# Block-sparse attention and an MLP mixer in one kernel: the gates of two batches computed transposed, in groups

## The chip, the cores and the metric

One core of a Trainium2 chip. A core has five engines that run side by side, each with its own queue: TensorE (PE: matmuls; its weight loads are listed as PEld), VectorE (DVE), ScalarE (ACT), GpSimd (POOL) and SyncE (SP), which here only issues transfers. 16 DMA engines move data between HBM (the main memory) and SBUF (the working memory, 128 partitions); TensorE writes to a third memory, PSUM. The metric is the device time of one execution in microseconds (us); the table below gives the median of four runs.

## The reference

Four batches, 8 heads, 768 positions, 64 values per head. Each query may see three of the 12 key blocks of 64 positions, chosen by a gate, and its own block, all of it causal. The result goes through a mixer of two MLPs: one across the 768 positions, one across the 512 channels.

```python
k_rep = k.reshape(B, H, 12, 64, D).mean(axis=3)
gate_scores = np.einsum('bhsd,bhnd->bhsn', q, k_rep)        # causal blocks only
top_idx = np.argsort(gate_scores, axis=-1)[..., -3:]
mask = chosen blocks | own block, and pos_q >= pos_k
attn = softmax(where(mask, scale * q @ k.T, -1e9))
x = (attn @ v), heads side by side                          # (4, 768, 512)
h = np.maximum(x.transpose(0, 2, 1) @ w_tok1, 0) @ w_tok2
u = x + h.transpose(0, 2, 1)
out = u + np.maximum(u @ w_ch1, 0) @ w_ch2
```

## The kernel before

**Pairs.** Two heads of a batch make a pair; there are 16 pairs, four to a batch. For pair i the kernel does the following.

- SP loads k, q and v (`load_qk` L265, two transfers each for k and q; `load_v` L274, one). The load buffers are rings: three for k, three for q (`kl`, `ql`), two for v.
- TensorE transposes k and q with six f32 transposes each (L353) into a PSUM tile `big`, ACT copies them to SBUF as `kt` and `qt` (L362), and GpSimd casts the halves to f16 into `KA` and `Q` (L368) and v into `V16` (L280). `KA` and `Q` have R = 4 slots, used in turn. Below or above the 64 head rows, each slot of `KA` holds 12 indicator rows (1 where a key lies in block n), and the matching 12 rows of `Q` get the mask's bias. So one matmul of 128 rows gives scores and mask together.
- DVE sums k over each block (`ksum` L376) and puts the sums of the two heads side by side into `ks2` (`kcopy` L384).
- The gate (L394): five f32 matmuls, each with 128 columns of `qt` as weights and the 24 columns of `ks2` streamed. DVE adds the causal bias (L402), takes the eight largest of each row of 12 with ten MAX8 (L411), compares with the third largest (L418), and makes the bias in f16, with the query's own block let through by `own` (L426, into `bn16`). TensorE transposes this bias, five f16 transposes (`mask` L437), and DVE copies the 12 rows of each head into `Q` (`put_mask` L445).
- Per head: scores in three tiles (L459), `exp` on ACT (L472), the diagonal blocks masked on DVE (L479; for pair 0 a triangle is added on TensorE, L463), the product with v (`av`, L490) and the normalisation on DVE (L498, L509) into `x16`.

**The MLP** of a batch follows when its four pairs are done: `tok1` (L521, L552 for batch 0), `umix` (L533, L566), the transpose of u (on TensorE for batch 0, by a DMA that SP issues for the others, L344), `ch1` (L602) with ReLU on ACT and DVE (L612, L614), `ch2` (L623), the last add (L631), the store (L635).

**The order.** Every step is an `Op` with an engine, a cost, dependencies, buffers and a priority. `plan()` makes the order of all engines from these before the program is emitted: each engine takes the ready step of the best priority. A pair's preparation has priority `pre = 10 (i - LATER)` (`AHEAD` for the first four), its attention 10 i, the MLP of batch b 1000 (b + 1), so MLP work is taken where attention has nothing ready. SP takes loads strictly by priority. Each engine's queue then runs in that fixed order. Ahead of it `manual_schedule` emits the set-up: constants over ACT's queue (`id32`, `gbias`, `own`, `id16`, `tri`), memsets on DVE and GpSimd, the indicator rows by GpSimd's queue (L875). The MLP weights are loaded by GpSimd's queue too, each behind the cast that `WAIT` names; `w_tok1` and `w_tok2` are the first. `dummy` matmuls (`warm`, L642) fill TensorE before 17 us. The path with `VIA` (k transposed by DMA) is in the code but off: `VIA = 16` is past the last pair.

Of the kernel before, what the change touches and what calls it, by code (L numbers as in the profile page):

```python
# [28 lines left out]
R = 4  # L29
# [3 lines left out]
VIA = 16  # L33
# [3 lines left out]
IDLE = 1e9  # L37
WAIT = [("kt", 3, 1), ("kt", 3, 1), ("qt", 3, 1), ("qt", 3, 1), ("qt", 4, 1), ("qt", 4, 1),
# [29 lines left out]
def plan(ops, rings, near=60.0):  # L68


    free = dict(PE=900.0, ACT=4800.0, DVE=4500.0, POOL=7500.0, SP=750.0, SPO=750.0)
# [106 lines left out]
def kernel(  # L178
# [26 lines left out]
    dram = ctx.enter_context(tc.tile_pool(name="dr", bufs=1, space=bass.MemoryType.DRAM))  # L205
# [3 lines left out]
    RINGS = dict(big=2, bank=3, av=1, ql=3, kl=3, v32=2, qt=2, kt=2, gs=2, e0=3, e1=3, e2=3, rc=2,  # L209
                 x16=3, h1=2, u=2, uT=2, h2=1, ob=3)  # L210
# [19 lines left out]
    K16 = [sp.tile([96, 8, 256], F16, tag=f"K16{y}", name=f"K16{y}") for y in range(2)]  # L230
    ks2 = [sp.tile([128, 2 * NB], FP, tag=f"ks{r}", name=f"ks{r}") for r in range(R)]
    bn16 = [sp.tile([128, NJ, 2, 64], F16, tag=f"bn{r}", name=f"bn{r}") for r in range(R)]
# [3 lines left out]
    wc2_16 = sp.tile([128, NFC, DM], F16, tag="wc2", name="wc2")  # L236
    warm = sp.tile([128, 256], F16, tag="warm", name="warm")
# [46 lines left out]
    def load_k8(i):  # L284
        b, h = pairs[i]

        def f():
            t = sb("kt", [128, 2, 8, D], FP, f"k8_{i}")[0:96]
            T["k8", i] = t
            nc.sync.dma_start(out=t.rearrange("p g t d -> p g (t d)"),  # L290
                              in_=k[b, h:h + 2].rearrange("g (p t) d -> p g (t d)", t=8))
        return f

    def ksum8(i):
        def f():
            t = sp.tile([96, 2, D], FP, tag="kp", bufs=2, name=f"kp_{i}")
            T["kp", i] = t
            nc.vector.tensor_reduce(out=t, in_=T["k8", i].rearrange("p g t d -> p g d t"), axis=AX.X, op=ALU.add)
        return f

    def ksum_pe(i):
        def f():
            p = ps("bank", [128, NB], "kps")
            T["kst", i] = p
            nc.tensor.matmul(out=p, lhsT=T["kp", i].rearrange("p g d -> p (g d)"), rhs=blk, start=True, stop=True)
        return f

    def cast_k8(i):
        def f():
            y = i % 2  # L310
            nc.gpsimd.tensor_copy(out=K16[y].rearrange("p t (g c) -> p g t c", g=4)[:, 0:4:3, :, :], in_=T["k8", i])
        return f

    def store_k(i):
        def f():
            t = dram.tile([S, 256], F16, tag=f"ks{i % 2}", name=f"kscr_{i}")
            T["kscr", i] = t
            nc.sync.dma_start(out=t.rearrange("(p t) c -> p (t c)", t=8), in_=K16[i % 2].rearrange("p t c -> p (t c)"))
        return f

    def turn_k(i):
        return lambda: nc.sync.dma_start_transpose(out=KAX[:, i % R, :, :], in_=T["kscr", i])

    def k16_zero(y):
        return lambda: nc.gpsimd.memset(K16[y].bitcast(FP), 0.0)

    def k16_ind(y):
        def f():
            for c in (64, 128):
                nc.gpsimd.tensor_copy(out=K16[y][:, :, c:c + NB],  # L330
                                      in_=blk.rearrange("p (o n) -> p o n", o=1).broadcast_to([96, 8, NB]))
        return f

    def zero_q(r):
        def f():
            nc.gpsimd.memset(QA[r][0][64:128, :].bitcast(FP), 0.0)
            nc.gpsimd.memset(QA[r][1][0:64, :].bitcast(FP), 0.0)
        return f

# [574 lines left out]
```

## Time and profile before

| what | value |
|---|---|
| median of 4 runs | 273.85 us (273.04 to 274.81) |
| the profiled execution's own time | 274.21 us |
| its span, first to last instruction | 272.4 us, granted clock 1.0 |
| busy PE / DVE / ACT / POOL | 261.6 / 162.1 / 142.3 / 81.3 us |
| gate matmuls L394 (80, recorded as 160) | 19.9 us busy |
| mask transposes L437 (80) | 7.1 us busy |
| HBM read | 27.21 MB |

Busy times of TensorE count each record from its start to its end, and records overlap, so what a matmul costs on the path is the distance between starts and is read from the chain of waits or from a timeline. "Idle before" in a group is the time in which its engine did nothing before an instruction of the group, with what ended it. The profiled execution is one run; it took 0.36 us more than the median.

### The profile page before, as it was taken

How to read it: one execution, taken by the hardware profiler on the slowest of the kernel's cores; microseconds unless marked ns; L12 is line 12 of the kernel's file. 1: busy time of each engine (PE TensorE's matmuls, PEld its weight loads, DVE VectorE, ACT ScalarE, POOL GpSimd, SP SyncE). 2: the span in 40 equal slices, each digit the busy share in tenths (PEclk: the TensorE clock that was granted, in tenths of full speed). 3: DMA queues.
4: the chain of work that ended last, by engine and by line, in shares of the span. 5: the costliest groups of instructions: out<-in, count | busy, mean ns of one | idle time of the engine just before them, and what ended most of it. 6: DMA issues, size and time to landing. Idle time of an engine off the chain costs nothing.

```text
span 272.4 us, 5924 instructions
## 1 busy us (share of the span) xinstructions
PE 261.6 (96%) x2309; PEld 173.9 (64%) x2309; DVE 162.1 (59%) x561; ACT 142.3 (52%) x188; POOL 81.3 (30%) x112
## 2 busy tenths in 40 slices
PE   7799879999999999999999999999999999999994
PEld 5687668886778777676877655644456544466443
DVE  5468947998889788889897633334233262433222
ACT  2366968877888888888477713430014400044000
POOL 8687807555445465337342000000000000000000
PEclk9999999999999999999999999999999999999999
DMA  8999999999999994581611111005420007210032
GB/s 174 199 215 218 150 210 215 199 185 198 222 213 226 204 213 97 110 182 25 117 41 41 38 43 75 0 2 103 145 99 2 0 16 177 84 73 0 2 143 88
DMA packets 92059, 32.31 MB, mean 119 GB/s; under 512 B 85568, under 2 KB 88536, under 8 KB 92032
## 3 DMA queue, kind: packets, MB, share of 16 engines
q1 hardware_dynamic: 87920, 27.53, 46.8%
q0 software_dynamic: 3392, 4.15, 9.2%
q8 instruction: 18, 0.29, 0.5%
q10 hardware_dynamic: 720, 0.25, 0.4%
q14 instruction: 9, 0.07, 0.1%
HBM read 27.21 MB, written 6.29 MB: 123 GB/s over the span
## 4 chain that ended last, share of the span: by engine, by line
PE 81%; DMA 8%; DVE 4%; SPq 2%; ACT 1%; issue 1%; POOL 1%; DVEq 0%; ACTq 0%; POOLq 0%
PE c L623 23%; PE c L602 22%; PE sps L459 10%; PE aps L490 6%; PE gps L394 5%; DMA ql<-in_q_dram 4%; PE ups L533 3%; PE tok L521 3%; PE tql L353 3%; DMA w<-in_moe_w_tok_dram 3%; PE tkl L353 3%; SPq L265 2%; DMA v<-in_v_dram 2%; PE bps L437 1%; ACT e L472 1%
## 5 line engine op out<-in xcount | busy, mean ns | idle before, releaser
L472 ACT ACTIVATE e<-sps 128x1024 f16<-128x1024 f32 (+1 forms) x96 | 84.3, 918 | 17.3 <-PE sps L459 11.9
L602 PE MATMUL c<-uT,wc 128*128 128x256 f16 (+1 forms) x384 | 68.1, 326 | 0.2 <-ACT h L612 0.2
L623 PE MATMUL c<-wc,h 128*128 128x512 f16 (+2 forms) x300 | 65.0, 371 | 0.0
L612 ACT ACTIVATE h<-c 128x512 f16<-128x512 f32 x48 | 28.7, 598 | 68.9 <-PE c L602 61.5
L602 PEld LDWEIGHTS <-wc 128*128 128x128 f16 x384 | 37.0, 98 | 24.6 <-issue 0.4
L459 PE MATMUL sps<-Q,KA 128*128 128x512 f16 (+3 forms) x256 | 50.0, 306 | 1.1 <-ACT e L472 1.0
L623 PEld LDWEIGHTS <-h 128*128 128x128 f16 x300 | 28.7, 98 | 31.4 <-issue 0.6
L614 DVE TENSOR_SCALAR h<-c 128x256 f16<-128x256 f32 x48 | 20.2, 421 | 33.8 <-PE c L602 33.8
L479 DVE TENSOR_TENSOR e<-e,m 128x256 f16<-128x256 f16 x90 | 31.8, 361 | 14.2 <-ACT e L472 13.7
L631 DVE TENSOR_TENSOR ob<-u,c 128x512 f32<-128x512 f16 (+2 forms) x25 | 16.6, 666 | 38.4 <-PE c L623 38.4
L368 POOL CAST KA<-kt 64x768 f16<-64x768 f32 x32 | 27.1, 848 | 28.3 <-ACT kt L362 24.9
L459 PEld LDWEIGHTS <-KA 128*128 128x128 f16 x256 | 22.5, 100 | 15.2 <-issue 1.1
L368 POOL CAST Q<-qt 64x768 f16<-64x768 f32 x32 | 26.7, 833 | 10.9 <-ACT qt L362 9.5
L490 PE MATMUL aps<-V,e 128*128 128x65 f16 x672 | 26.9, 194 | 0.3
L490 PEld LDWEIGHTS <-e 128*128 128x128 f16 x672 | 25.6, 98 | 2.2 <-issue 0.4
L394 PEld LDWEIGHTS gps<-ks,qt 128*128 128x128 f32 x160 | 19.2, 192 | 2.5 <-DVE ks L384 1.3
L280 POOL CAST V<-v 128x768 f16<-128x768 f32 x16 | 13.2, 827 | 25.1 <-DMA v<-in_v_dram 21.0
L394 PE MATMUL gps<-ks,qt 128*128 128x24 f32 x160 | 19.9, 267 | 0.3 <-DVE ks L384 0.2
L362 ACT COPY kt<-tkl 128x768 f32<-128x768 f32 x16 | 12.8, 798 | 11.1 <-PE tkl L353 5.7
L509 DVE TENSOR_TENSOR x<-aps,rc 128x384 f16<-128x384 f32 x32 | 17.6, 550 | 0.5
L445 DVE COPY Q<-bps 12x640 f16<-12x640 f16 x32 | 15.5, 484 | 1.9 <-PE bps L437 0.7
L362 ACT COPY qt<-tql 128x768 f32<-128x768 f32 x16 | 12.8, 798 | 7.0 <-PE tql L353 6.3
(55 smaller groups left out, 217.0 us busy)
## 6 DMA issues: line engine op xcount, KB each, us to landing
kl<-in_k_dram SPq DMA_DIRECT2D x32, 192.0 KB, 5.0
ql<-in_q_dram SPq DMA_DIRECT2D x32, 192.0 KB, 4.6
v<-in_v_dram SPq DMA_DIRECT2D x16, 384.0 KB, 5.4
out_dram<-ob SPq DMA_DIRECT2D x23, 256.0 KB, 2.0
wc<-in_moe_w_ch_dram POOLq DMA_DIRECT2D x8, 384.0 KB, 7.8
w<-in_moe_w_tok_dram POOLq DMA_DIRECT2D x2, 384.0 KB, 8.3
out_dram<-ob SPq DMA_DIRECT2D x1, 160.0 KB, 1.8
KA<-indc POOLq DMA_DIRECT2D x2, 72.0 KB, 4.4
```

The costliest lines, as they stand in the source:

```text
L362: nc.scalar.copy(out=t, in_=p[:, 0:S])
L368: nc.gpsimd.tensor_copy(out=dst[i % R][x][lo:lo + 64, :], in_=T[name, i][lo:lo + 64, :])
L394: nc.tensor.matmul(out=g[:, j, :], lhsT=T["qt", i][:, 128 * j + 128:128 * j + 256], rhs=ks2[i % R], start=True, stop=True)
L459: nc.tensor.matmul(out=p[:, off + a:off + a + n], lhsT=KA[i % R][x][:, 128 * kk:128 * kk + 128], rhs=QA[i % R][x][:, q0 + a:q0 + a + n], s ...
L472: nc.scalar.activation(out=e[:, 0:width], in_=T["sps", i, x, g][:, 0:width], func=AF.Exp, scale=scale)
L479: nc.vector.tensor_tensor(out=d, in0=d, in1=m0, op=ALU.mult)
L490: nc.tensor.matmul(out=p[:, jq, :], lhsT=T["e", i, x, g][:, o:o + 128], rhs=V16[i % (R + 1)][:, x, kk, :], start=(kk == 0), stop=(kk == jq))
L509: nc.vector.tensor_tensor(out=T["x16", b][:, :, 64 * hh:64 * hh + 64], in0=T["aps", i, x][:, :, 0:64], in1=T["rc", i, x].broadcast_to([128 ...
L602: nc.tensor.matmul(out=p, lhsT=wc1_16[:, cc, 128 * fc:128 * fc + 128], rhs=T["uT", b][:, cc, a // 128:e // 128, :], start=(cc == 0), stop= ...
L612: nc.scalar.activation(out=T["h2", b][:, fc, a:e], in_=T["c1", b, fc, n], func=AF.Relu)
L614: nc.vector.tensor_scalar(out=T["h2", b][:, fc, a:e], in0=T["c1", b, fc, n], scalar1=0.0, scalar2=None, op0=ALU.max)
L623: nc.tensor.matmul(out=T["c2", b, j, lo], lhsT=T["h2", b][:, fc, 128 * j:128 * j + 128], rhs=wc2_16[:, fc, lo:hi], start=(fc == 0), stop=( ...
```

## The change

Pairs 0 to 5 keep their gates one by one. Pairs 6 and 7 make a group, 8 to 11 another, 12 to 15 a third (`GROUPED`). For a group the gate is turned round: `ks2` of a pair (24 columns, padded to 32) is the weight and 640 columns of `qt` are streamed, in two matmuls (512 and 128 columns). Pair s of the group uses columns 32 s to 32 s + 31 of the array (`tile_position`) and so writes partitions 32 s and up. ACT copies the result to SBUF (`gate_e`), five f32 transposes turn it back (`gate_b`), and one add, one comparison and one bias serve the group; MAX8 stays at ten per pair. The biases lie packed, 32 columns a pair, in `bn16`, so five f16 transposes give the masks of the whole group. `put_mask` now copies 24 rows (both heads), and the indicator rows of head 1 lie 12 rows further, so that each head picks its own.

With it: R becomes 5, `qt` has four buffers, `x16` two in place of three, `bn16` four in a ring of its own; the bias works on `own4`, in which `own` stands four times; preparation of a group has one priority base (2.5 apart for its pairs, `EXTRA` 5 earlier), v keeps its old one; the code of the `VIA` path goes, with its constant `blk`. In the set-up only slot 0 of `KA` is cleared and gets the indicators from DMA; slots 1 to 4 are copied from it on GpSimd in `zero_q`, which also fills `own4`, except for its first part, which DVE copies behind its memsets of `ks2`.

```diff
-R = 4
+R = 5
+NBN = 4
+EXTRA = 5.0
+GATE = {2: 1150, 3: 1400, 4: 1700}
+GROUPED = [[0], [1], [2], [3], [4], [5], [6, 7], [8, 9, 10, 11], [12, 13, 14, 15]]
...
     RINGS: qt=2 -> 4, gs=2 -> 1, x16=3 -> 2, new: gt=1, gm=1, m8=1, bn=NBN
...
     def zero_q(r):
         def f():
+            for x in range(2):
+                lo = 64 * (1 - x)
+                nc.gpsimd.tensor_copy(out=KAX[lo:lo + 64, r, x, :].bitcast(FP), in_=KAX[lo:lo + 64, 0, x, :].bitcast(FP))
             nc.gpsimd.memset(QA[r][0][64:128, :].bitcast(FP), 0.0)
             nc.gpsimd.memset(QA[r][1][0:64, :].bitcast(FP), 0.0)
+            if r < 4:
+                nc.gpsimd.tensor_copy(out=own4[:, r:4 * GJ:4, :], in_=own)
...
+    def gate_t(gi):
+        def f():
+            p = ps("big", None, "gtp")
+            T["gtp", gi] = p
+            for a, e in ((0, 512), (512, S - 128)):
+                for s, i in enumerate(GROUPED[gi]):
+                    nc.tensor.matmul(out=p[32 * s:32 * s + 32, a:e], lhsT=ks2[i % R],
+                                     rhs=T["qt", i][:, 128 + a:128 + e], start=True, stop=True,
+                                     tile_position=(0, 32 * s))
+    def gate_e(gi):
+            nc.scalar.copy(out=t[0:n, :], in_=T["gtp", gi][0:n, 0:S - 128])
+    def gate_b(gi):
+            for j in range(GJ):
+                nc.tensor.transpose(out=p[:, 128 * j:128 * j + n], in_=T["gt", gi][0:n, 128 * j:128 * j + 128],
+                                    identity=ident32[0:n, 0:n])
...
+    def mask(gi):
+            for j in range(GJ):
+                nc.tensor.transpose(out=p[0:n, 128 * j:128 * j + 128], in_=bn16[gi % NBN][:, j, 0:n], identity=ident16)
-            nc.vector.tensor_copy(out=QA[i % R][x][lo:lo + NB, 128:S], in_=T["bps", i][lo:lo + NB, :])
+            nc.vector.tensor_copy(out=QA[i % R][x][lo:lo + 2 * NB, 128:S], in_=T["bps", gi][32 * s:32 * s + 2 * NB, :])
...
-        pre = 10.0 * (i - (AHEAD if i < FIRST else LATER))
+        pre = 10.0 * (i0 - (AHEAD if i < FIRST else LATER)) + 2.5 * (i - i0) - (0 if len(GROUPED[gi]) == 1 else EXTRA)
+        vpre = 10.0 * (i - (AHEAD if i < FIRST else LATER))
...
         for r in range(R):
             nc.vector.memset(ks2[r], 0.0)
+        nc.vector.tensor_copy(out=own4[:, 0:4 * GJ:4, :], in_=own)
         for x in range(2):
             lo = 64 * (1 - x)
-            for r in range(R):
-                nc.gpsimd.memset(KAX[lo:lo + 64, r, x, :].bitcast(FP), 0.0)
+            nc.gpsimd.memset(KAX[lo:lo + 64, 0, x, :].bitcast(FP), 0.0)
...
-        blk = const("blk", (np.arange(96)[:, None] // 8 == nidx[None, :]).astype(np.float32), FP, nc.gpsimd)
```

The new order keeps TensorE's queue as it was up to the gate of pair 5, apart from the size of the masks. From there on the transposes of pairs 7 and 9 to 15 come earlier; on SP, k and q of pair 7 stand ahead of v of pair 5, k and q of pairs 9 to 11 ahead of v of pairs 7 to 10, and k and q of 12 to 15 ahead of v of 11.

## The prediction

> **What bounds the kernel now.** I read the page's slices first, then the table of stages, then the chain of waits, then the groups of the gate. The slices (TensorE, its granted clock, DMA):
>
> ```profile
> PE   7799879999999999999999999999999999999994
> PEclk9999999999999999999999999999999999999999
> DMA  8999999999999994581611111005420007210032
> ```
>
> TensorE is full from the sixth slice (34 us) to the last one, at full clock; DMA is full for the first 14 slices (95 us). The stage table (stretch, length, busy us of PE, PEld, DVE, ACT, POOL, clock, DMA share, GB/s) says the same with numbers:
>
> ```profile
> 30.00:40.00 10.00, 7.79 (x122) 5.88 (x121) 6.15 (x21) 7.80 (x11) 3.30 (x5) 1.00 1.16 191
> 60.00:70.00 10.00, 9.72 (x125) 7.25 (x123) 8.30 (x33) 7.88 (x11) 5.63 (x7) 1.00 1.13 199
> 90.00:100.00 10.00, 9.95 (x112) 7.79 (x110) 7.57 (x31) 8.97 (x13) 4.24 (x6) 1.00 1.02 205
> 120.00:130.00 10.00, 10.00 (x105) 7.03 (x103) 9.89 (x37) 8.71 (x10) 5.38 (x6) 1.00 0.40 79
> 260.00:272.40 12.40, 8.74 (x53) 4.74 (x51) 2.81 (x5) 0.00 (x0) 0.00 (x0) 1.00 0.29 105
> ```
>
> From 40 us on TensorE idles some 0.5 us up to its last matmul at 268.5 us, because MLP matmuls of finished batches fill what attention leaves. So after 40 us a microsecond of TensorE work saved is a microsecond off the end, whatever ACT or DVE do, as long as no wait takes its place. Before 40 us there is nothing to fill with, and the chain of waits (start, length, what) runs through loads and GpSimd:
>
> ```profile
> 20.91 5.16 DMA v<-in_v_dram
> 26.19 0.84 POOL V L280
> 27.08 0.74 POOL KA L368
> 27.96 0.77 POOL Q L368
> 28.74 7.47 DMA w<-in_moe_w_tok_dram
> 36.25 0.84 PE tok L552 x12
> ...
> 81.21 1.08 PE gps L394 x10
> ```
>
> **The gate, per pair.** The groups by form (busy, mean ns of one, idle before):
>
> ```profile
> L394 PE MATMUL gps<-ks,qt 128*128 128x24 f32 x160 | 19.9, 267 | 0.3 <-DVE ks L384 0.2
> L353 PE MATMUL tkl<-id,kl 128*128 128x128 f32 x96 | 13.3, 275 | 0.7 <-issue 0.7
> L437 PE MATMUL bps<-id,bn 128*128 128x128 f16 x80 | 7.1, 220 | 0.1
> ```
>
> 160 records for 80 gate matmuls: an f32 matmul that is no transpose goes through as two. On the path a gate is 1.08 us (chain above; 1.03 to 1.30 over the pairs) and the five mask transposes 0.28 us. For pairs 6 to 15 that is 10 x 1.08 + 10 x 0.28 = 13.6 us of TensorE, all removed.
>
> **What replaces it on TensorE.** Three groups: a pair and two fours. No row shows column tiles, nor a long f32 stream, so I bound both. Stream: six f32 transposes take 0.66 us, 110 ns for 128 columns or 0.86 ns a column; two records per matmul make 1.72 ns, so 640 columns are 1.10 us (the old gate passed the same 640 columns as weights in 1.08 us). Lowest end: the f16 row, 512 columns each 216 ns, which gives 0.27 us. Overlap of the tiles: from full (one stream) to none (n streams). Each tile's loads I put at 0.1 us (an f32 load of 128 columns is 192 ns, and 32 columns take less; two records). I take full overlap, 1.10 + 0.1 n plus 0.1: 1.3 us for the pair, 1.6 us for a four, since the tiles share neither weights nor output partitions; the other end, no overlap, is 2.4 and 4.8 us. Turning back is five f32 transposes, 0.55 us a group, and a mask 0.28 us a group. Sum: 1.3 + 1.6 + 1.6 + 3 x 0.55 + 3 x 0.28 = 7.0 us. **Saved on TensorE: 6.6 us**; without overlap 0.9 us is lost (2.4 + 4.8 + 4.8 + 2.5 = 14.5 us); at the f16 rate 9.1 us are saved.
>
> A record of a 128x512 f16 matmul lasts 379 ns while the next starts 216 ns later, so 0.16 us of each is tail that the next one covers. The Trainium skill (TensorEngine Tiling (Array Packing), Key Properties) says that a change of tiling mode drains TensorE. By that rule each group would pay the tail on entering and on leaving, 6 x 0.16 = 1.0 us, and the forecast below would be 270.7 instead of 269.7; no row here shows such a switch.
>
> **ACT and DVE.** Three evacuations of 640 columns come to ACT: by the 768-column copy (798 ns) about 0.7 us each. DVE's gate chain shrinks: add, compare and bias of four pairs cost 4 x 0.86 us (277, 305, 278 ns), and at 480 elements about 0.65 us each by the 512-element add of 688 ns. Both are covered by TensorE's fill. But the chain of a four is now one long latency ahead of four pairs: add 0.65, forty MAX8 3.3, compare 0.67, bias 0.65, with some 2 us of other DVE work queued between (reciprocal, output add, two ReLUs, a diagonal), 7.2 to 7.6 us in all. In the new order TensorE has 8.7 us of work between turning back and mask for pairs 8 to 11, and 7.15 us for 12 to 15. I charge **0.5 us** of wait for the second (0 to 1.5).
>
> **Loads, moved on SP's queue.** k and q of pair 7 now go ahead of v of pair 5, those of 9 to 11 ahead of v of 7 to 10. In that stage DMA is the limit (199 GB/s), so a load moves by what it overtakes: v is 0.39 MB, 1.9 us. q of pair 7 was issued at 55.25 and landed 9.9 us later, 65.1; it will land at 63.2. TensorE's new order wants it 6.8 us after the gate of pair 5 (54.5 us), at 61.3, or 62.7 with the late start below: **0.5 us** of wait (0 to 2.5). k of pair 8 overtakes nothing (71.8 us) and is wanted at 72.1; q of pair 8 about 74.5, wanted at 75.0. TensorE took these three about 5 us after they landed (69.97, 76.8 and 78.98 us); now it is under one. k of 11 gains 5.7 us and is early. v of 9 and 10 wait for the two v buffers, with k and q of 12 queued behind them on SP; by bytes k of 12 stays where it was (landed near 95), wanted at 95.6.
>
> **The start.** Timeline of the first microseconds (start, length, engine, what):
>
> ```profile
> 0.75 3.00 POOL L865 MEMSET KA<- 64x384 f32 x8 [0.29 <-POOLq L898]
> 1.91 0.49 ACTq L214 DMA_DIRECT2D own<-ownc  x1
> 6.05 0.96 DVE L376 TENSOR_REDUCE kst<-tkl 128x12 f32<-128x768 f32 x1 [2.02 <-PE tkl L353]
> 7.05 0.80 ACT L362 COPY kt<-tkl 128x768 f32<-128x768 f32 x1 [4.80 <-DMA tri<-tric]
> ```
>
> DVE now copies `own` before most of its memsets, and `own` lands at 6.1 us (4.2 after issue). Behind that wait stand two Q memsets, four bn16 memsets and six V16 memsets, 2.5 us, then the block sums of pair 0: 6.05 becomes about 8.9, ACT's copies wait for that, and the first scores move from 15.0 to about 16.0. GpSimd loses six KA memsets (2.2 us) and gains, per further ring slot, two KA copies (0.41 each, by the memset of the same shape at 1.07 ns an element, as the 768-element cast; 0.82 at most) and an `own` copy (0.2, three times), and a whole fifth slot. Its queue: the indicator DMA lands near 6.6, slots 1 and 2 until 10.6, pair 0's casts until 14.1, then with slots 3 and 4 in between without a gap to the issue of `w_tok1` at 30.1 in place of 28.74. The kernel before left GpSimd 3.5 us of idle between 11 and 27 us (1.10, 1.00, 0.42, 0.59 and 0.43 ahead of its casts), so only 1.4 us of its added work shows. TensorE already waits for this load, so `tok` starts near 37.6 instead of 36.25: **1.4 us lost**, which contains the 1.0 us of the first scores. With copies at 0.82 it is 4.6 us; if DMA, not the issue, times that load, 0.5 us. The dropped `blk` load (0.5 us of GpSimd) is in this.
>
> **Sum.** -6.6 + 0.5 + 0.5 + 1.4 = -4.2 us. The profiled execution took 274.21 us (span 272.4 and 1.8 around it), 0.36 above the median 273.85 and inside the runs' spread (273.04 to 274.81). 274.2 - 4.2 = 270.0; on the median **269.7 us**.
>
> **Rivals.** (a) *The tiles run one after the other.* Then the three gates cost 12.0 instead of 4.5 us, 7.5 us more: 277.2 us, slower. For it: no row here shows two matmuls side by side. Against it: distinct weights, outputs and streams. It decides from the point where the three gates together exceed 8.7 us, about 3.2 us for a four. (b) *They overlap in twos*: 2.6 us a four, 271.7 us. (c) *A wait takes the place*: GpSimd's copies at 0.82 (3.2 us more: 272.9), or the k and q of pairs 7 and 8 late by 2 us and more and the mask chain late in both fours (also about 3 us). For it: margins under 1 us and a full DMA; against it: every one of these is met by the counts above. (d) *Nothing of the start shows and the tiles cost just one stream*: 7.7 saved, 0.5 to 1 lost: 267.0 us. (e) That the gates were hidden anyway and nothing changes I exclude: TensorE is full where they stand.
>
> **How the numbers follow.** Forecast 0.50 (its own range 268.3 to 271.3), (d) 0.10, (b) 0.10, (c) 0.15 (272 to 274.5), (a) 0.15 (274.5 to 278). Range 267.0 to 275.0: below it half of (d), above it most of (a). Measurement tells 0.5%, 1.4 us: faster is below 272.5, slower above 275.2. Faster: 0.50 + 0.10 + 0.08 + 0.06 = 0.74; slower 0.12, from (a) and a little of (c) with it; within 0.14.
>
> **What would show it.** Right: one tiled gate of four spanning 1.2 to 1.9 us, its matmul records overlapping; 0.55 us for turning back; `tok` of batch 0 near 37.6; TensorE full from 40 us; waits on q of pair 7 under 1 us. Wrong: a tiled gate over 3 us, TensorE idle in 57 to 76 us on k or q loads, idle ahead of the masks near 105 or 145 us, or the first `tok` past 39 us.

## The result, and the profile after

The changed kernel takes 273.57 us (median of 54 runs, 270.47 to 278.83), the kernel before 273.47 us (78 runs beside them, 272.51 to 278.37). Over all runs the medians are the same within 0.1 us, where a gain of 4.2 us was forecast. The ratio is 0.997, with an interval of 0.9956 to 0.9984; like all ratios below it is formed only from runs within 1.5% of the fastest of their kernel, which here leaves out 16 of the 54 and 2 of the 78. The profiled execution took 271.72 us (span 270.0, full clock) against 274.21 (span 272.4) before: between these two it is 2.5 us. So there are two gaps to explain: 4.2 against 2.5 us in the profile, and 2.5 us against nothing between the profile and the median of the runs.

The slices of the page (TensorE, its granted clock, DMA) have dips that the kernel before did not have, in slices 13 and 14 of DMA (6 and 4) and in 15 and 18 of TensorE (7 and 6):

```profile
PE   6798999999999979969999999999999999999994
PEclk9999999999999999999999999999999999999999
DMA  8999999999996499967412000006320026310032
```

In the table of stages (columns as in the prediction) they have their sizes. TensorE's busy time from 90 to 120 us was 29.9 of 30 us before (the row of 90 to 100 us stands in the prediction; before, then after):

```profile
100.00:110.00 10.00, 10.00 (x110) 7.68 (x110) 8.45 (x35) 8.51 (x12) 5.95 (x8) 1.00 0.64 137
110.00:120.00 10.00, 9.95 (x105) 7.14 (x103) 7.76 (x28) 8.15 (x11) 4.12 (x5) 1.00 0.51 112
```

```profile
90.00:100.00 10.00, 8.49 (x87) 5.70 (x86) 6.34 (x24) 6.65 (x10) 7.14 (x9) 1.00 0.64 136
100.00:110.00 10.00, 9.80 (x83) 6.83 (x82) 7.68 (x43) 5.11 (x7) 3.63 (x4) 1.00 1.21 223
110.00:120.00 10.00, 7.58 (x59) 4.17 (x58) 9.89 (x19) 6.05 (x8) 5.76 (x7) 1.00 0.91 183
```

After the change that is 4.1 us of idle time. The whole account, from the same table summed over the span:

| us | before | after | difference |
|---|---|---|---|
| TensorE busy | 261.6 | 256.3 | -5.3 |
| TensorE idle up to 40 us | 6.4 | 5.6 | -0.8 |
| TensorE idle from 40 us to its last matmul, and the end | 4.4 | 8.1 | +3.7 |
| span | 272.4 | 270.0 | -2.4 |

What the change was meant to do, it does. TensorE's timeline around the gate of pairs 8 to 11 (start, length, what; in brackets the idle time before it and its releaser):

```profile
94.86 1.28 PE L361 MATMUL gtp<-qt,ks 128*32 128x512 f32 x16
96.08 0.45 PE L455 MATMUL sps<-Q,KA 128*128 128x512 f16 x2
96.36 0.60 PE L598 MATMUL c<-uT,wc 128*128 128x256 f16 x4
96.96 0.77 PE L381 MATMUL gbp<-id,gt 128*128 128x128 f32 x5
99.24 0.85 PE L310 MATMUL tkl<-id,kl 128*128 128x128 f32 x6 [1.51 <-DMA kl<-in_k_dram]
```

Sixteen matmul records in four column tiles take 1.22 us until the next work starts. The pair takes 1.20 (from 65.42 to 66.62), the second four 1.22 (140.67 to 141.89). Twice the tiles add 0.02 us: they overlap fully. But the last line is the first new wait: TensorE waits for k of pair 12. It comes from SP's queue (its timeline; the length is from the first to the last issue of the group):

```profile
78.80 13.83 SPq L276 DMA_DIRECT2D v<-in_v_dram  x4
92.72 1.79 SPq L267 DMA_DIRECT2D kl<-in_k_dram  x2
94.61 2.81 SPq L267 DMA_DIRECT2D ql<-in_q_dram  x2
```

SP stands for 13.8 us at four loads of v, because v of pairs 9 and 10 needs the two v buffers, and GpSimd's casts of v of 7 and 8 free them late (the casts start at 86.1 and 91.4 us). Meanwhile DMA has less to do: slices 13 and 14 of its row fall to 6 and 4. The second new wait is near 118 us, first in TensorE's timeline, then in that of VectorE:

```profile
116.18 0.23 PE L486 MATMUL aps<-V,e 128*128 128x65 f16 x2
116.70 0.27 PE L486 MATMUL aps<-V,e 128*128 128x65 f16 x3 [0.30 <-DVE e L475]
118.95 0.68 PE L486 MATMUL aps<-V,e 128*128 128x65 f16 x16 [1.99 <-DVE e L475]
```

```profile
109.26 4.00 DVE L441 COPY Q<-bps 24x640 f16<-24x640 f16 x8
113.29 0.69 DVE L537 TENSOR_TENSOR u<-x,ups 128x512 f16<-128x512 f16 x1
113.90 2.75 DVE L475 TENSOR_TENSOR e<-e,m 128x256 f16<-128x256 f16 x2
116.57 0.94 DVE L333 TENSOR_REDUCE kst<-kt 128x12 f32<-128x768 f32 x1
117.43 1.27 DVE L537 TENSOR_TENSOR u<-x,ups 128x512 f16<-128x512 f16 x2
118.62 0.48 DVE L475 TENSOR_TENSOR e<-e,m 128x256 f16<-128x256 f16 x2
```

The packed mask of four pairs is ready all at once, so its eight copies into Q stand in one row, 4.00 us, where before two at a time were spread over four pairs. Behind them come two diagonals (L475) of 1.15 and 1.68 us, against a median of 0.29 us for the 90 in this profile, and the third diagonal of pair 8, for which TensorE waits, has a block sum and two u adds ahead of it. The two slow diagonals are 2.2 us longer than usual together, as much as the wait itself. They lie beside six GpSimd casts without a pause (113.3 to 118.2 us). The Trainium skill (GPSIMD Engine Reference, Specifications) says that GpSimd shares its memory interface with VectorE, and that VectorE instructions with two inputs in SBUF contend for it; the trace agrees with that: the 62 of the 90 diagonals with no GpSimd work beside them took 0.294 us at most, and every longer one overlapped some (though not every one that did was longer).

At the start, `own` holds up VectorE as forecast (the chain has 4.59 us of `own` from 1.90 us on; the sum of block 0 begins at 9.2 us, forecast 8.9), and the first gate waits:

```profile
11.71 1.29 PE L351 MATMUL gps<-ks,qt 128*128 128x24 f32 x10 [1.85 <-ACT qt L319]
36.51 0.83 PE L548 MATMUL tok<-x,w 128*128 128x128 f16 x12
```

But the first token matmul starts at 36.51, 0.26 us later than before, not 1.35: `w_tok1` was issued at 30.5, 1.8 us later, and landed 5.7 us after its issue instead of 7.5 (at 36.26 us, before at 36.20).

**Between the profile and the runs.** Each of the 54 runs carries its mean granted clock:

```
mean clock of the run     runs   median us
0.998 to 1.000              11      271.64
0.994 to 0.996              12      272.86
0.988 to 0.992              13      273.73
0.984 to 0.987               6      274.48
0.972 to 0.981              12      276.40
```

A straight line through them gives 271.45 us at full clock and 2.4 us more for each per cent of clock (correlation 0.92). The profiled execution is one of the fastest fifth, with full clock. The kernel before varies less: the middle 80% of its runs lie within 272.7 to 274.8, those of the changed kernel within 271.5 to 276.4. And its clock hardly varies: of 68 runs of it that were taken beside the experiments with their clocks, 66 have 0.997 or more and none less than 0.994. At 0.998 and more the medians are 271.64 us for the changed kernel (11 runs) and 273.56 for the one before (60 runs). So the change gives 1.9 us at full clock, and the clock takes as much from the changed kernel's median; the other 0.7 us of the profile's 2.5 is that the profiled execution before lay 0.7 us above its median.

### The profile page after: what moved, and what is told of

Same layout as the page of the kernel before. It is cut to its first block, busy times and chain, and to the rows that moved or that the text cites. A ratio compares the mean times of both kernels' runs of the same rounds, so it can differ in the third digit from the quotient of the medians.

```text
span 270.0 us, 5718 instructions
## 1 busy us (share of the span) xinstructions
PE 256.3 (95%) x2229; PEld 164.0 (61%) x2229; DVE 161.0 (60%) x544; ACT 141.5 (52%) x191; POOL 83.9 (31%) x118
## 4 chain that ended last, share of the span: by engine, by line
PE 85%; DVE 7%; DMA 3%; ACT 2%; issue 1%; ACTq 0%; SPq 0%
PE c L598 23%; PE c L619 22%; PE sps L455 13%; PE aps L486 8%; PE tql L310 3%; PE tkl L310 3%; PE ups L529 3%; PE tok L517 2%; PE gps L351 2%; DMA own<-ownc 2%; DMA ql<-in_q_dram 2%; DVE Q L441 1%; ACT e L468 1%; PE gtp L361 1%; PE bps L434 1%; DVE e L475 1%
## 5 line engine op out<-in xcount | busy, mean ns | idle before, releaser
L455 PE MATMUL sps<-Q,KA 128*128 128x512 f16 (+3 forms) x256 | 49.0, 306 | 1.0 <-ACT e L468 1.0
L619 PEld LDWEIGHTS <-h 128*128 128x128 f16 x300 | 28.8, 98 | 30.5 <-issue 0.6
L325 POOL CAST KA<-kt 64x768 f16<-64x768 f32 x32 | 26.3, 823 | 47.9 <-ACT kt L319 34.8
L475 DVE TENSOR_TENSOR e<-e,m 128x256 f16<-128x256 f16 x90 | 30.9, 352 | 14.9 <-ACT e L468 14.2
L325 POOL CAST Q<-qt 64x768 f16<-64x768 f32 x32 | 27.4, 856 | 4.2 <-ACT qt L319 2.8
L505 DVE TENSOR_TENSOR x<-aps,rc 128x384 f16<-128x384 f32 x32 | 17.7, 553 | 0.7
L333 DVE TENSOR_REDUCE kst<-kt 128x12 f32<-128x768 f32 x15 | 14.2, 945 | 4.0 <-ACT kt L319 3.7
L441 DVE COPY Q<-bps 24x640 f16<-24x640 f16 x32 | 15.4, 483 | 1.3 <-PE bps L434 0.7
L310 PE MATMUL tkl<-id,kl 128*128 128x128 f32 x96 | 13.3, 275 | 2.6 <-DMA kl<-in_k_dram 1.5
```

Source lines behind the costliest of these rows:

```text
L310: nc.tensor.transpose(out=p[:, 128 * j:128 * j + 128], in_=t[:, j, :], identity=ident32)
L325: nc.gpsimd.tensor_copy(out=dst[i % R][x][lo:lo + 64, :], in_=T[name, i][lo:lo + 64, :])
L441: nc.vector.tensor_copy(out=QA[i % R][x][lo:lo + 2 * NB, 128:S], in_=T["bps", gi][32 * s:32 * s + 2 * NB, :])
L455: nc.tensor.matmul(out=p[:, off + a:off + a + n], lhsT=KA[i % R][x][:, 128 * kk:128 * kk + 128], rhs=QA[i % R][x][:, q0 + a:q0 + a + n], s ...
L475: nc.vector.tensor_tensor(out=d, in0=d, in1=m0, op=ALU.mult)
L619: nc.tensor.matmul(out=T["c2", b, j, lo], lhsT=T["h2", b][:, fc, 128 * j:128 * j + 128], rhs=wc2_16[:, fc, lo:hi], start=(fc == 0), stop=( ...
```

## The experiments

**Theory.** Most of the missing gain is two waits from the new order: (1) k and q of pair 12 behind v on SP; (2) VectorE's eight copies and what stands behind them. Rivals: the waits only pass the time on to each other; the rest of the change (masks, start) costs more than the forecast has; and it is the clock (TensorE's granted clock falls in some runs behind an idle time).

**k and q of pair 12 ahead of v of 9 and 10** (inserted in the planned order):

```diff
+    hold = next(o for o in order if o.prio == 82.0 and o.eng == "SP")
+    for key in (("kl", 12), ("ql", 12)):
+        order.remove(O[key])
+        order.insert(order.index(hold), O[key])
```

> The changed kernel; only on SP's queue k and q of pair 12 stand ahead of v of pairs 9 and 10. Theory A (the gain went into two waits of TensorE: 1.5 and 0.2 us for k and q of pair 12, held on SP behind v of 9 and 10, which wait for their buffers until GpSimd has cast v of 7 and 8; and 2.3 us for the diagonals of pair 8 on DVE): the first wait goes, k of pair 12 lands before 95 us, the span is 1.5 to 2 us shorter (268.0 to 268.5 at full clock). Rival B (the second wait grows by what the first one gives, since the mask chain of pairs 8 to 11 sets both): span within 0.5 us of 270.0. Theory C (the granted clock falls in some runs after an idle stretch of TensorE of 1.5 us or more): runs below clock 0.99 become fewer, the mean clock of the runs rises; if the clock falls for another reason, it stays at about 0.99.

Measured: 273.87 us (5 runs, 270.03 to 277.66), ratio 0.9943 (0.9879 to 1.0008). The wait for k of pair 12 is gone from the table of waits, the wait for the diagonal stays at 2.4 us (the profiled run had a clock of 0.944, so only its waits are read). The time decides nothing by itself. The clocks of the five runs (0.944 to 0.994) did not rise, as the theory of the clock expected.

**The third diagonal of pair 8 ahead of the block sum and the u adds:**

```diff
+    order.remove(O["dg", 8, 0, 2])
+    order.insert(order.index(O["dg", 8, 0, 1]) + 1, O["dg", 8, 0, 2])
```

> The changed kernel; only on DVE's queue the third diagonal of pair 8 stands ahead of the block sums of pair 14 and two adds of u. Theory A: the wait of 2.0 us of the first product with v of pair 8 shrinks to 0.3 to 0.6 us (two diagonals of 1.1 and 1.7 us still stand before it), span 268.3 to 268.8 at full clock. Rival B (another instruction of DVE's queue takes over, such as the adds of u that hold MLP tiles): span within 0.5 us of 270.0. Theory C: one idle stretch fewer, so the mean clock of the runs rises.

Measured: 273.4 us (10 runs), ratio 0.9994 (0.9956 to 1.0031). The table of waits (us in total, times, longest):

```profile
PE aps L486 <- DVE x L505: 1.8, 1, 1.8
PE tkl L310 <- DMA kl<-in_k_dram: 1.6, 1, 1.6
```

The wait for the diagonal is gone, and a wait of 1.8 us for the normalisation of pair 8 (L505) stands in its place: one edit in VectorE's order passes the time on to the next thing in that queue.

**Both together:**

> Both edits of the two runs before. Theory A: their gains add up, span 266.3 to 267.0 at full clock, which is 5.5 us under the kernel before and about what was forecast for TensorE's work plus the start. Theory C: no idle stretch of TensorE over 0.7 us is left past 40 us, so the clock is 1.0 in nearly all runs and the median is within 1 us of the fastest run, 268 to 269 us. If C is wrong, half the runs stay 2 us and more above the fastest.

Measured: 271.32 us (5 runs, 271.06 to 271.76), ratio 0.9932 (0.9912 to 0.9953). Wait (1) is gone, and the normalisation takes 2.3 us. Both theories missed here: the span is 269.7 us and not 266.3 to 267.0, and all five runs have a clock of 0.992 to 0.994 where 1.0 was expected. The profile has one stretch of 3.4 us at half clock, from 13.1 us on, behind the wait of 1.6 us for the first gate: the waits of the middle are not the only ones that matter for the clock.

**The copies of nine to eleven and thirteen to fifteen left out**, on top of both edits (12 of 32 copies; the masks of six pairs are then not applied):

```diff
+            if len(GROUPED[gi]) == 4 and s > 0:
+                return
```

> The run with both edits, and in the two groups of four only the first pair's mask rows are copied: twelve of the 32 copies of mask rows (24 rows x 640, 0.48 us each on DVE) are left out, so the output is not the reference's. Theory A2 (what is left of TensorE's wait in 115 to 123 us, 2.3 us ahead of a product with v, is DVE's backlog behind eight copies in a row, 4.0 us): the wait falls under 0.5 us and the span by 1.5 to 2.5 us against the run with both edits. Rival (the backlog is the six adds of u and GpSimd's casts at the same time, the copies only stand near it): the wait stays above 1.5 us.

Measured: 267.78 us (4 runs, 267.61 to 268.81), ratio 0.9786 (0.9739 to 0.9833), span 265.5 against 269.7 us. TensorE from 105 to 125 us is busy 18.97 us instead of 17.25, so 1.7 of the 4.2 us come from here. The rest lies at the start, where the profiled run with the copies waits 1.6 us for the first gate and has its stretch at half clock, which this run has not. The wait fell to 1.0 us, between the theory (under 0.5) and the rival (over 1.5). So wait (2) comes mostly with the row of copies. Part of that may be the slow diagonals: with the copies the first three of pair 8 stand beside the casts and take 2.95 us, without them they come ahead of most of the casts and take 0.28, 0.29 and 0.43 us. What the copies cost of themselves and what they cost by pushing the diagonals beside the casts, no run here separates.

**All gates single**, the rest of the change kept:

```diff
-GROUPED = [[0], [1], [2], [3], [4], [5], [6, 7], [8, 9, 10, 11], [12, 13, 14, 15]]
+GROUPED = [[n] for n in range(16)]
```

> The changed kernel with all 16 gates one by one as before; ring of 5, set-up, packed masks and buffers stay, and the plan orders it anew. It tells what the grouping alone gives. Theory A (grouping saves 7 us of TensorE and its long order gives 4 us back in waits): the waits in 95 to 120 us are gone, gates and masks cost 13.6 us again for pairs 6 to 15, and the time is within 1.5 us of the kernel before, 272.5 to 275, about the same as the changed kernel. Rival (grouping works as forecast and the rest of the change costs the difference): 276 us and more.

Measured: 276.56 us (4 runs, 276.46 to 276.84), ratio 1.0096 (1.0059 to 1.0133), as the rival has it. No new wait near 100 or 118 us, but TensorE is busy 264.6 us instead of 261.6. The gates and masks are the same in number as before; only the mask transposes now take 32 columns of the mask and so run in column tiles. TensorE's timeline around one mask, before and then with single gates:

```profile
65.70 0.60 PE L602 MATMUL c<-uT,wc 128*128 128x256 f16 x4
66.19 0.45 PE L437 MATMUL bps<-id,bn 128*128 128x128 f16 x5
66.48 0.43 PE L459 MATMUL sps<-Q,KA 128*128 128x512 f16 x2
```

```profile
66.42 0.60 PE L598 MATMUL c<-uT,wc 128*128 128x256 f16 x4
66.95 0.45 PE L434 MATMUL bps<-id,bn 128*32 128x128 f16 x5
67.33 0.45 PE L455 MATMUL sps<-Q,KA 128*128 128x512 f16 x2
```

Before, the mask starts 0.11 to 0.17 us ahead of the modelled end of the matmuls before it, and the next work 0.28 to 0.29 us after it; in tile mode 0.07 ahead, and 0.38 to 0.39 after. Over all 16 masks the medians are -0.16 and 0.28 against -0.07 and 0.39 us: 0.20 us for each mask, 0.09 going in and 0.11 coming out, 3.2 us for 16. By this count that would be the whole of the 3.05 us, but 0.4 us of these are the dummy matmuls of the start, which take 8.9 us instead of 8.4 (from each start to the next), so at most 2.6 are left for the masks. The sizes of instruction records do not show it (221 ns against 220).

**Masks of 128 columns**, in the changed kernel and in the one with single gates:

```diff
-                nc.tensor.transpose(out=p[0:n, 128 * j:128 * j + 128], in_=bn16[gi % NBN][:, j, 0:n], identity=ident16)
+                nc.tensor.transpose(out=p[:, 128 * j:128 * j + 128], in_=bn16[gi % NBN][:, j, :], identity=ident16)
```

> The changed kernel, with one thing undone: the mask transposes take all 128 columns of the packed mask (weights of 128*128), not the 32 or 64 of the group, so TensorE does not go into a column-tile mode and out of it for them. In the trace of the changed kernel a mask group of five in tile mode starts 0.07 us before the end of the matmuls ahead of it, where one of 128 columns starts 0.16 before it (the rows of before, and of the groups of four), and the next work starts 0.38 to 0.39 us after it, where it starts 0.28 after one of 128 columns: 0.20 us for each group in tile mode. There are seven such groups, two of them inside the idle time of the start. Theory: 5 x 0.20 us plus at most 2 x 0.10 goes, 1.0 to 1.2 us; span 270.0 to about 268.9, ratio to before about 0.993. Rival: what is ahead of the waits for k of pair 12 and for VectorE's diagonals is lost again in them, since both are set by other queues: the wait for k of pair 12 grows from 1.5 to 2.5 us and the span stays within 0.3 us of 270.0, ratio 0.997.

> The kernel with all gates single, which took 276.56 us (ratio 1.0096), and with masks of 128 columns. Against before it keeps the packed masks' layout, the copies of ks on other rows, and the copy of own4 at the start. Theory: mode changes are the whole of what it lost, 16 groups x 0.20 us = 3.2 us: 273.4 us, ratio 0.998 to 1.001, TensorE busy back from 264.6 to 261.6 us. Rival: the start (first gate 2 us later, first token stage later) has a share of it: 274.5 us, ratio 1.003 to 1.005, and TensorE's idle time in the first 40 us is over that of before by 1 us.

Measured for the changed kernel: 272.0 us (6 runs, 269.74 to 276.37), ratio 0.9906 (0.987 to 0.9943). The mask groups are like those of before (medians -0.16 and 0.28), the mask of pairs 8 to 11 starts at 107.60 instead of 108.34, and the span is 270.1 as against 270.0 us: TensorE's idle time from 110 to 125 us grew to 2.8 us. At equal clock the span is as the rival has it, what the masks give is lost again ahead of VectorE; the two runs at full clock take 271.17 and 271.89 us, against 271.64 for the changed kernel. The gain that the median shows is less than the spread of these six runs, and I do not count it.

With single gates: 275.71 us (10 runs, ratio 1.0065, 1.0042 to 1.0088); the profiled run took 385.9 us at a clock of 0.658, which nothing here explains. Better by 0.85 us, not by 3.2, and 2 us from the kernel before. The next run asks where these are.

**Single gates, masks of 128 columns, and `own` copied behind the other work of the start** (one line moved from ahead of the memsets to behind them):

> The kernel with all gates single and masks of 128 columns, which took 275.71 us (ratio 1.0065), with own4 copied on VectorE behind the other work of the start. Theory: the rest of what it lost to before is the start, where VectorE stands at own until 6.5 us and the first gate waits; TensorE's idle time before 20 us then falls from 4.3 to under 3.5 us, as before has it, and the time comes to 273.5 to 274.3 us, ratio 1.000 to 1.003. Rival: the rest lies elsewhere (GpSimd's queue, the copies of the masks): 275.0 us or more, ratio 1.005 or more.

Measured: 275.3 us (10 runs, 274.12 to 277.07), ratio 1.0055 (1.0023 to 1.0087). The idle time before 20 us fell to 2.4 us, under that of before (3.4), and yet the time hardly moved: by its time the rival holds. The profile names something else. The masks are like those of before (medians -0.16 and 0.28), no wait past 40 us is over 0.6 us, and TensorE is busy 263.8 us. Of these, one stretch that begins in the first token matmul's wait for its weights ran at half clock (0.95 of full clock in 32 to 36 us, 0.62 in 36 to 40), which costs up to 1.7 us. Without it the sum is 262.1 busy and 10.4 idle, 272.5 us: the kernel before (272.4). But that compares two single executions, and the runs do not bear it out. At a clock of 0.998 and more, the medians lie above the kernel before in the same set of runs by 3.2 us with single gates (4 runs), by 1.4 us with wide masks as well (5 runs), and by 0.9 us with `own` later too (6 runs). So the masks and the start account for 2.3 of the 3.2 us; the 0.9 us that stay are there at full clock, and their cause is open.

**`own` copied later, in the changed kernel:**

```diff
-        nc.vector.tensor_copy(out=own4[:, 0:4 * GJ:4, :], in_=own)
...
             nc.vector.memset(V16[r][:, :, :, 64:65], 1.0)
+        nc.vector.tensor_copy(out=own4[:, 0:4 * GJ:4, :], in_=own)
```

> The changed kernel; only DVE's copy of own into own4 stands behind its memsets instead of before them, so the block sums of pair 0 start near 6.9 instead of 9.2 us and TensorE's idle time ahead of the first gate (1.6 to 2.1 us, near 10 us) shrinks to under 0.5 us. Theory C2 (two of the four profiles so far show the granted clock at one half for one stretch of 3.4 us that begins 1.1 to 1.3 us after this idle time; such stretches, here and behind the waits in 97 to 119 us, are what lowers the mean clock of the runs, 1.7 us each at most): the profile shows no half-clock stretch before 20 us; the times at the upper end thin out and the median falls by 0.7 to 1.7 us, to about 272. Rival (the start is hidden by the wait for w_tok1, and the clock falls for reasons of the chip): median within 0.5 us of 273.4, spread as before.

Measured: 272.37 us (10 runs, 269.9 to 274.54), ratio 0.9923 (0.988 to 0.9966). TensorE is busy 9.24 us from 10 to 20 us, 8.12 in the changed kernel. This profile (span 270.8) shows where the clock goes. A table of stages behind wait (2), where TensorE stood idle for 2.0 us until 118.2:

```profile
116.00:118.00 2.00, 0.22 (x3) 0.09 (x3) 2.00 (x4) 0.33 (x1) 1.41 (x2) 1.00 1.10 244
118.00:119.00 1.00, 0.79 (x15) 0.80 (x16) 1.00 (x4) 0.00 (x0) 0.89 (x1) 0.63 0.81 149
119.00:120.00 1.00, 1.00 (x9) 0.60 (x7) 0.89 (x4) 0.00 (x0) 0.04 (x1) 0.50 0.15 58
120.00:121.00 1.00, 1.00 (x5) 0.47 (x4) 0.35 (x3) 0.85 (x1) 0.00 (x0) 0.50 0.98 241
121.00:122.00 1.00, 1.00 (x14) 0.54 (x13) 0.15 (x1) 1.00 (x2) 0.00 (x0) 0.67 1.17 267
```

The clock is 0.50 for 3.4 us and then full again. TensorE does half its work in that time, so the stretch costs 1.7 us, beside the 2.0 us of the wait.

**Both orders and the later `own`:**

> Both edits of loads and diagonal, and the start edit. Theory C2: no half-clock stretch at the start, clock 1.0 in the profile, median 269.3 to 270.3 us, ratio to the kernel before 0.985 to 0.989. If the start does not matter, 271.3 us as with the two edits alone.

Measured: 271.0 us (10 runs, 269.58 to 273.41), ratio 0.992 (0.9884 to 0.9955). The profiled run was the slowest of the ten and has two such stretches, one from 36.4 us at the end of a wait of 1.6 us for `w_tok1` and one from 121.8 us behind the 2.4 us for the normalisation. The median lies between the two forecasts (269.3 to 270.3, and 271.3), so how much the start matters is not settled by it.

**A gap of 2 us in the kernel before**, near 228 us, where its TensorE is never idle (two matmuls with a chain of copies on ACT between them):

> The kernel before, with one idle stretch of TensorE put into the last batches' MLP, near 205 us: one small matmul, four copies on ACT one after the other, and a matmul that needs the last of them, some 2.2 us of idle in which nothing else waits. Theory C: besides its own 2.3 us, some runs show a granted clock under 0.995 and lie another 2 us and more higher; in the profile, if it is such a run, the clock is lower in the 10 us behind the gap. Rival (the clock falls because of the tiled matmuls or the later start): all runs keep clock 1.0 and lie 2 to 2.5 us above the kernel before.

Measured: ratio 1.0157 (1.0117 to 1.0197), from two of the four runs, 276.89 and 278.01 us. Of the others the profiled one took 282.73 us at a clock of 0.949, and one took 956.44 us, which nothing here explains. No stretch at half clock follows this gap in the profile, so an idle time of 2 us does not always bring one. The two runs behind the ratio say more: they lie 3.5 and 4.6 us above the median beside them (273.37 us, 15 runs with clocks of 0.997 and more), and their clocks, 0.994 and 0.993, are lower by what one stretch of 3.4 us at half clock takes off (0.006 of the span). That is what the theory of the clock expected, and a clock of 1.0 with 2 to 2.5 us more, the rival, did not come. They are only two, and where in them the stretch lies is not known.

**A better version: both orders, the later `own`, masks of 128 columns, and the copies of the four cut in two.** `Again` turns the mask of the group a second time, and the copies of pairs 10 and 11 come from there, behind the u adds:

```diff
+    late = [O["put", m, x] for m in (10, 11) for x in range(2)]
+    for o in late:
+        order.remove(o)
+    at = order.index(O["uadd", 1, 5]) + 1
+    order[at:at] = late
+    order.insert(order.index(O["umix", 1, 5]) + 1, Again())
```

> The changed kernel with four edits: loads of k and q of pair 12 ahead of v of 9 and 10, third diagonal of pair 8 earlier, own4 copied behind the other work of the start (these three took 271.0 us together, ratio 0.992), masks of 128 columns, and the eight copies of the mask of pairs 8 to 11 cut in two: the mask is turned a second time (0.28 us of TensorE) after the last token matmul of batch 1, and the four copies for pairs 10 and 11 come from that, behind the u adds. Theory: VectorE's eight copies in a row make the wait of 2.3 us near 118, and mode changes cost 1.0: the wait falls below 0.5 us, and the time is 271.0 - 1.8 - 1.0 + 0.3 = 268.5 us, ratio about 0.982. Rival: VectorE is full from 113 to 124 us in any case, and the four copies only move the wait to the scores of pair 10, near 125: a wait of 1 to 2 us there, 269.8 to 270.2 us, ratio 0.988.

Measured: 269.6 us (6 runs, 268.62 to 271.92), ratio 0.9859 (0.982 to 0.9898), span 266.8 us at full clock. Its table of waits:

```profile
PE aps L485 <- DVE e L474: 1.8, 1, 1.8
PE aps L485 <- DVE x L504: 1.2, 2, 1.0
```

The time forecast was 268.5 us. The four copies moved the wait to the next diagonal, as the rival has it, but the span is 3.2 us below that of the changed kernel.

**The same with the copies and the block sum of pair 14 placed behind pair 9's diagonals and its normalisation:**

```diff
+    moved = [(("put", 10, 0), ("dg", 9, 1, 1)), (("put", 10, 1), ("put", 10, 0)),
+             (("ksum", 14), ("norm", 9, 1)), (("kcopy", 14), ("ksum", 14)),
+             (("put", 11, 0), ("kcopy", 14)), (("put", 11, 1), ("put", 11, 0))]
```

> The version of four edits that took 269.6 us (span 266.8), with its work on VectorE near 115 to 125 us in another order: the four mask copies of pairs 10 and 11 stand behind the diagonals of pair 9 (10) and behind the normalisation of pair 9 (11), with the sum of k of pair 14 (0.95 and 0.33 us) between them instead of in pair 8. Theory: the order on VectorE makes the two waits left there (1.75 us for the third diagonal of pair 9, behind four copies, and 0.99 us for the normalisation of pair 8, behind the sum and the u adds); both fall below 0.5 us and the span to 264.5 us, time about 267.3 us, ratio 0.978. Rival: VectorE has too much to do between 108 and 125 us in any order: a wait of over 1.5 us comes back before the scores of pair 10 or 11, and the time stays at 269 us or above, ratio 0.984 or more.

Measured: 269.73 us (6 runs, 268.4 to 272.45), ratio 0.9851 (0.98 to 0.9902), span 266.9 us. The waits near 118 us:

```profile
PE aps L485 <- DVE e L474: 0.9, 2, 0.7
PE aps L485 <- DVE x L504: 0.5, 2, 0.3
```

They are 1.4 us together instead of 3.0, so the order, not the amount, of VectorE's work made most of them. The span (264.5 forecast) did not follow, because this execution waited in its first 40 us for DMA (1.0 us each for k and q, 0.9 for `w_tok1`), and was busy there 34.7 us against 36.2 in the run above, with the same code at the start. Which of the two versions is faster is not settled. Both take 1.4 to 1.5% less than the kernel before, where the changed one takes 0.3% less.

## Why the prediction was wrong

- **What bounds the kernel:** right. TensorE's work fell, and what the span did not gain of it past 40 us stands as new idle time of TensorE, 3.7 us, in waits that can be named. That busy and idle time add up to the span proves nothing, as they always do; that a wait on TensorE is span shows in the run without the twelve copies, where 1.7 us of it went and the span fell. (The slices were read one off: TensorE is full from the seventh, 41 us, and DMA for the first 15, 102 us; and at the f16 rate the sum gives 9.0 us saved, not 9.1. Nothing hangs on either.)
- **What replaces the gate on TensorE:** right in kind, and the tiles better than taken: 1.20, 1.22 and 1.22 us against 1.3, 1.6 and 1.6; turning back 0.45 for the pair and 0.55 for the second four against 0.55. That the overlap would be full was a choice between two bounds, and it came true. Rivals (a) and (b) are out.
- **Saved on TensorE, 6.6 us:** 5.3 measured in busy time. Counted from each start to the next, gates, turning back and masks take 6.7 us less (21.9 and 15.2), so the size was met, in part by luck: the tiles were 0.9 us better than taken, and the term missed what the diff shows in one place, that masks of single pairs also take 32 columns now. Seven mask groups outside the fours, at 0.20 us, are 1.4 us, of which about 0.8 lie in the masks and 0.6 ahead of them (an estimate from the medians above). Another 0.7 us are the dummy matmuls of the start, 9.1 us instead of 8.4; they are no work, and without them TensorE's work fell by 6.0 us. The rule of the Trainium skill that I weighed and left out (TensorEngine Tiling (Array Packing), Key Properties: a change of tiling mode drains TensorE) fits what was measured: a price of 0.09 us in and 0.11 us out, paid by the masks, which I had not counted as tiles. That a drain is what costs it, no run shows; that the price is gone with masks of 128 columns, two runs do.
- **The loads:** the step that failed first. "By bytes k of 12 stays where it was (landed near 95)" holds only for a queue that is never stopped. The same sentence says that v of 9 and 10 wait for buffers with k and q of 12 behind them, and prices that at nothing: k of 12 landed at 99.1 us, and it cost 1.7 us of waits (1.5 and 0.2), with DMA at 40 to 60% meanwhile. The charge of 0.5 us for q of pair 7 was not needed, no wait for it is in the table.
- **ACT and DVE:** the step that failed most. "Both are covered by TensorE's fill" was said of the chain ahead of the mask, and there it holds: no four waits for its mask. What comes behind the mask, eight copies in one row, was in the diff and was not counted: 2.3 us of waits. It also pushed two diagonals beside GpSimd's casts, where they took 2.2 us longer than usual.
- **The start, 1.4 us lost:** mechanism right (`own` delays the first sums and the first gate by 2 us), size wrong: TensorE's idle time up to 40 us fell by 0.8 us, but 0.7 of that is filled with dummy matmuls, so the start cost nothing and gave nothing (idle and dummies 14.8 us before, 14.7 after). `w_tok1` landed when it had landed before, 5.7 us after an issue that was 1.8 us later: the bound "if DMA, not the issue, times that load, 0.5 us" was the nearer one. Across the runs the wait for that load is anything from 0 to 1.6 us, so this term has an uncertainty as large as itself.
- **Sum:** -4.2 forecast, -2.4 in the profile: TensorE's work 0.6 us short (6.0 for 6.6), the mid-run waits 2.7 us worse (3.7 for 1.0), the start 1.5 us better (-0.1 for +1.4). Without that last error the sum would have missed by more.
- **From profile to runs:** the forecast moved its sum from the profiled execution to the median as if both kernels lose alike to the clock. They do not: the runs of the kernel before stay at 0.997 and more, while the changed kernel's median run has a clock of about 0.99, worth 1.9 us. What I can show is that stretches at half clock stand behind waits of 1.6 to 2.4 us in several profiles, among them one of the waits that the change made, and that its runs vary more than those of before. By their clocks its 54 runs have from none to about four such stretches (3.4 us at half clock lowers the mean by 0.006, and 2.4 us for a per cent makes that 1.5 us a stretch, near the 1.7 of the trace). How many lie at 118 us and how many at the start is not known, as only one execution of each kernel is profiled.
- **Rival (c), a wait takes the place,** had the right form at 272.9 us and was given 0.15; "every one of these is met by the counts above" was said of the waits named, and two others came. "TensorE idle on loads" and "idle ahead of the masks near 105" were looked for in the right region, but not at the place. That the measured time lies near the rival's number is luck: none of the waits that it names came.

## What to carry to other kernels

When work of several steps is packed into one, look behind the packed step, not only ahead of it: what was spread (here copies, two at a time) falls in one row on some engine, and whatever was queued behind the first pair of them is now late. A load that waits for a buffer stops the loads that stand behind it on its queue (SP stood for 13.8 us here, with DMA down to 40%), so count the release of that buffer, not only the bytes. And before an operand is cut to the columns that are needed, see whether that puts TensorE into tile mode: the 128-column form of the same transposes was cheaper by 0.20 us a group. And before one profile is compared with a median, look at the clock of every run: the same change was 2.5 us faster in the profiles, 1.9 us at full clock and nothing in the median.

## What the runs showed of the hardware that I had not expected

Idle times of 1.6 to 2.4 us were enough, some of the time, for 3.4 us at half clock (0.50), which costs up to another 1.7 us. Four profiles have such a stretch within 1.8 us of the end of one (a fifth has it behind two waits of 0.6 and 1.0 us, 2 us apart), while several idle times of 2 us have none. The Trainium skill (TensorE: Matmul & The Clock Gate, What's actually happening) gives a free-running window of 3413 ns, which is the length seen here, and throttling after an idle window of about 3.4 us; here shorter idle times preceded it.

Which waits are followed by it, the clock records of the traces narrow down. Within each profile the changes of the clock lie whole multiples of 3.413 us apart, so the clock is granted by fixed stretches of that length, and a wait falls into them as it happens to lie. An estimate of how full TensorE's matmuls make each of these stretches (0.42 ns for a column streamed in f16 and 0.86 ns in f32, from the rows in the prediction) gives 0.21 to 0.37 for the six that stand just ahead of one at half clock. All others in these profiles up to the last matmul are at 0.41 or more, but for one at 0.36 in the profile of the gap, which runs at 0.949 throughout (the profile at 0.658 is left aside). The wait of 2.0 us near 118 us lies in a stretch filled to 0.22 in the run with `own` later, which half clock follows, and mostly in one filled to 0.46 in the changed kernel, which it does not follow. So it goes with how empty one such stretch is, and not with the length of a wait alone. This was found in the traces afterwards, and no run tests it.
